# A fused attention and two-layer kernel: attention products three steps later, weight sums in place, output slots and splits at fixed places

## The chip, the cores and the metric

One core of one Trainium2 chip. The metric is the device time of one execution in microseconds (us), the median over the runs. Engines: PE is TensorE's matmul, PEld its weight load, DVE is VectorE, ACT is ScalarE, POOL is GpSimd, SP is SyncE, which issues nearly all DMA transfers here. Each engine works through its own queue in program order.

## What is computed

q, k and v are [8, 8, 576, 64] float32 (drawn as 0.1 times a normal; q and k times about 4.3). Within chunks of 64 rows:

```python
scores = scale * np.matmul(q_c, k_c.transpose(0, 1, 2, 4, 3))
scores = scores - np.max(scores, axis=-1, keepdims=True)
attn = np.exp(scores)
attn = attn / (np.sum(attn, axis=-1, keepdims=True) + 1e-09)
out = np.matmul(attn, v_c)
```

Heads are then laid side by side, which gives x of [4608, 512], and two layers follow, with weights of 512 x 2048 and 2048 x 512 that arrive as float64:

```python
h = x @ w_in                                                # layer one
x = (np.maximum(h, 0.0) + alpha * np.minimum(h, 0.0)) @ w_out
h = x @ w_in2                                               # layer two
out = (h - np.tanh(h)) @ w_out2
```

## The kernel before

**Precision.** Each float32 operand of a large product is split into a high part (a ScalarE copy into float32r, the type that PE takes) and a low part (operand minus high part, on VectorE or GpSimd); a product is hi*hi + lo*hi + hi*lo, three matmuls for one. The float64 weights are turned into float32 by bit operations (`to_f32_a` on ScalarE, L115 and L118; `to_f32_op` on VectorE, L128 to L138).

**Steps (layer one, blocks 0 to 6).** The 4608 tokens form nine blocks of 512. The first seven go through layer one in 112 steps, one for each block and slice of 128 of the 2048 hidden values. A step (`step_one`, L1008 on) holds twelve matmuls `up` (L525) into a PSUM bank `hps` (two exist), the gate (`act_g`: ScalarE L536 and L537, VectorE L538), the split of the last step's gate (L553, L556), and twelve matmuls `down` (L595) for the gate of two steps earlier. Everything else is hung into steps by a table of events: `at(step, fn, ..., place=)`. `fire` runs the places 0 to 4 of a step: 1 and 2 ahead of `up`, 0 between `up` and `down`, 3 after `down`, 4 after the gate. So each engine's queue is written by hand.

**Attention inside the steps.** A tile is 128 tokens with all eight heads. For a tile t with `base[t] = s`: raw q and k come by many small DMAs (`begin_unit`, `some_loads`, L318; for four tiles in the natural layout, L284) and are transposed on VectorE (`att_a`, L363) or, natural ones, on PE; scores at s (`att_s`, L378), maximum, subtraction and exponential at s + 1 (`att_e`), normalization at s + 2 (`att_n`), the transpose of the weights (`att_t`, L428) and their copies into the single buffer `ptb` (`att_d`: four on VectorE, L437, four on ScalarE, L438) at the end of s + 2, and the product with v (`att_v`, L449) at s + 3. One step later the result is copied out as a split operand (`att_x`, L495 and L499) or, for the last two blocks, staged and stored (`att_x_out`, L511). Scores and products share one pair of PSUM banks: the products of one tile stand beside the scores of another (`beside`). The raw buffer is single, and its next loads begin when the last transpose has read it. `base` holds a gap of three steps between most tiles and of four at four places.

**Parked weights.** From step 36 on, in rounds of four steps, seven sums and differences of weight quarters for each pair of hidden slices are formed, split and stored to DRAM (`wu`) for the later cycles, in two halves c = 0 and 1. `park_form` forms layer one's ("u1") from the resident split weights on GpSimd (L215, L221) and layer two's ("u") from a converted raw load; `park_split` splits (L238 on ScalarE, L239 on GpSimd); `park_store` issues two DMAs (L244). Both kinds use the one buffer `mr` of tag "r"; the raw load and the high part take the two buffers of tag "w". In a round the u1 form stands at the end of step 0, its split at the end of step 1, its store in step 2; the u load in step 1, its form at the end of step 2, its split at the end of step 3, its store in step 4. From step 100 on the second layer's `w_out2` slices ("d") follow, six in the steps and ten in the cycles.

**Cycles (`two_blocks`).** The last two blocks of layer one (s = 0) and layer two's blocks in pairs (s = 1 to 4) use seven products for eight: a cycle (s, p) makes p1, p5, p6, p2, p3, p7, p4 (six matmuls each, L1168) for a pair of blocks and a pair of hidden slices. Weights come through a ring of eight buffers (`fetch_up`, L260). VectorE makes the sums H1 = X + p5 and Y = X + p5 in PSUM (`add`, L1175); H1 is the operand of the bank that p3 goes on with. Four gates of a cycle run on ScalarE (`Gate.square`, `second`, `edge`: L568 to L580) and VectorE (`drain`: L573, L574, from PSUM; `close`: L584 to L586, from SBUF). Gated values wait in a list `line` of units, half of them by way of DRAM; `downs(n)` issues n matmuls of the front unit's twelve (L1084). Sizes of these runs are in `gaps`, 24 matmuls a cycle for s = 0 and 48 for s >= 1. A unit's values are split (L553, then L556 on GpSimd) when a unit begins, for the two first of the line, and the third in the middle. When the last unit of a block ends, four banks are copied out (`put_bank`, L620, three buffers of tag "st" in turn) and the next block's first unit begins in the same banks; for s >= 1 that is in the cycles p = 0 and p = 4. `border` hangs the next pair's operands into places of a cycle: loads (`load_y`), differences (`tokens`, L688), split copies (`put`, L676, L678). `small` does the last block at half width. Working buffers of 128 x 512 come from a list of some twenty slots (`take`, first in first out).

## Time and profile before

| what | us |
|---|---|
| runs: median (lowest to highest of 3) | 1808.88 (1802.18 to 1812.13) |
| the profiled execution | 1804.53 |
| its span, first to last instruction | 1802.8 |
| PE / PEld busy | 1656.1 / 1351.9 |
| DVE / ACT / POOL busy | 1302.5 / 994.8 / 469.6 |
| DMA: 276.51 MB moved, mean | 153 GB/s |

The profile is of one execution. Busy time is the union of an engine's instructions. "PEclk" or "clock" is the share of TensorE's full clock (2.4 GHz) that was granted in a stretch; the lower level is 1.2 GHz. A wait is the idle time of an engine before an instruction, put down to what ended it ("<-"). The timeline merges equal instructions in a row (xN). "SPq" are DMA issues on SyncE's queue. A tile's name is that of the program; one name can stand for several buffers.

### The profile page before, as it was taken

The page shows a single profiled execution, that of the slowest core. Times are in us where ns is not written, and L with a number is a line of the kernel's source. Part 1 is how long each engine was busy: PE and PEld are TensorE (multiplying, and loading weights), DVE is VectorE, ACT ScalarE, POOL GpSimd, SP SyncE. Part 2 cuts the span into 40 slices and gives each one's busy share as a digit, 9 for nine tenths or more (in the row PEclk, how much of TensorE's full clock was granted, in tenths as well). Part 3 has the DMA queues.
Part 4 walks back from the last instruction along what each step waited for, and adds up shares of the span by engine and source line. Part 5 has one row for each costly group of instructions (what it writes and reads, how often), then busy time and mean ns, then how long its engine had stood idle before and what let it go on. Part 6 is the DMA issues. An engine that isn't in the chain of part 4 may idle for free.

```text
span 1802.8 us, 26393 instructions
## 1 busy us (share of the span) xinstructions
PE 1656.1 (92%) x9309; PEld 1351.9 (75%) x9309; DVE 1302.5 (72%) x1860; ACT 994.8 (55%) x1785; POOL 469.6 (26%) x406
## 2 busy tenths in 40 slices
...
GB/s 252 184 138 39 97 99 117 128 140 104 136 94 126 128 117 140 154 146 197 230 239 234 292 238 101 185 147 176 111 184 137 176 123 175 136 155 141 224 170 24
DMA packets 345061, 276.51 MB, mean 153 GB/s; under 512 B 180048, under 2 KB 250720, under 8 KB 344928
## 3 DMA queue, kind: packets, MB, share of 16 engines
...
q14 instruction: 59, 0.48, 0.1%
...
## 4 chain that ended last, share of the span: by engine, by line
PE 39%; DVE 12%; DMA 6%; ACT 6%; issue 5%; SPq 3%; POOL 2%; DVEq 0%; ACTq 0%; POOLq 0%
PE y L1084 18%; PE hpb L1168 11%; PE hps L1168 6%; PE y L595 3%; SPq L318 3%; DMA wu<-mr 2%; PE hps L525 2%; DVE arena L585 2%; DVE arena L584 1%; DMA out_dram<-yst 1%; ACT sq L568 1%; DVE arena L573 1%; ACT w L577 1%; DVE th L574 1%; DMA wu<-wu 1%
## 5 line engine op out<-in xcount | busy, mean ns | idle before, releaser
L556 POOL TENSOR_TENSOR glo<-arena,ghi 128x512 fp32r<-128x512 f32 x142 | 206.0, 1455 | 519.0 <-ACT ghi L553 437.2
L525 PE MATMUL hps<-x,w 128*128 128x512 f32 (+1 forms) x1356 | 328.7, 392 | 4.5 <-ACT kt L352 3.8
L1084 PE MATMUL y<-w,ghi 128*128 128x512 f32 x1152 | 301.3, 395 | 10.1 <-ACT yst L620 10.1
L525 PEld LDWEIGHTS hps<-x,w 128*128 128x128 f32 x1356 | 255.8, 190 | 58.8 <-ACT kt L352 4.2
L1168 PE MATMUL hpb<-w,wu 128*128 128x512 f32 (+1 forms) x1200 | 284.4, 380 | 8.5 <-DVE th L574 5.1
L1168 PEld LDWEIGHTS hpb<-w,wu 128*128 128x128 f32 x1200 | 218.5, 190 | 55.5 <-DVE th L574 8.1
L1084 PEld LDWEIGHTS y<-w,ghi 128*128 128x128 f32 x1152 | 217.6, 191 | 56.4 <-ACT yst L620 12.2
L595 PE MATMUL y<-ghi,w 128*128 128x512 f32 x880 | 250.2, 420 | 0.0
L595 PEld LDWEIGHTS y<-ghi,w 128*128 128x128 f32 x880 | 174.5, 203 | 39.0
L1168 PE MATMUL hps<-w,wu 128*128 128x512 f32 (+1 forms) x624 | 143.1, 373 | 25.2 <-DVE hps L1175 24.8
L1084 PE MATMUL y<-w,glo 128*128 128x512 f32 x576 | 163.7, 391 | 0.0
L556 DVE TENSOR_TENSOR glo<-g,ghi 128x512 fp32r<-128x512 f32 x111 | 111.8, 1008 | 68.9 <-ACT ghi L553 68.8
L239 POOL TENSOR_TENSOR mr<-mr,whi 128x896 fp32r<-128x896 f32 (+1 forms) x48 | 93.4, 1946 | 256.1 <-ACT whi L238 247.0
L1168 PEld LDWEIGHTS hps<-w,wu 128*128 128x128 f32 x624 | 109.2, 191 | 52.9 <-DVE hps L1175 33.8
L586 DVE COPY_PREDICATED arena<-ktc,th 128x512 f32<-128x512 uint32 x126 | 132.8, 1054 | 11.4 <-ACT ktc L580 0.6
L538 DVE SCALAR_TENSOR_TENSOR g<-neg,nalpha_sb,g 128x512 f32<-128x512 f32 x112 | 92.5, 826 | 60.2 <-ACT g L537 60.2
L595 PE MATMUL y<-glo,w 128*128 128x512 f32 x440 | 130.2, 400 | 1.0 <-DVE glo L556 1.0
L1084 PEld LDWEIGHTS y<-w,glo 128*128 128x128 f32 x576 | 108.4, 189 | 22.5
L585 DVE SCALAR_TENSOR_TENSOR arena<-sq,arena 128x512 f32<-128x512 f32 x126 | 116.6, 926 | 4.3
L221 POOL TENSOR_TENSOR mr<-mr 128x128 f32<-128x128 f32 x128 | 72.7, 578 | 154.4 <-DVE mr L138 140.0
L536 ACT ACTIVATE neg<-hps 128x512 f32<-128x512 f32 x112 | 65.9, 589 | 75.8 <-PE hps L525 75.1
L577 ACT ACTIVATE w<-sq,bias_sb 128x512 f32<-128x512 f32 x144 | 104.5, 726 | 0.0
...
## 6 DMA issues: line engine op xcount, KB each, us to landing
...
```

Source lines behind the costliest of these rows:

```text
L221: nc.gpsimd.tensor_tensor(out=mr[:, o], in0=mr[:, x], in1=mr[:, y], op=op)
L239: nc.gpsimd.tensor_tensor(out=lo.bitcast(F32R), in0=m, in1=h.bitcast(F32), op=ALU.subtract)
L525: nc.tensor.matmul(out=hp[:, cols], lhsT=w[:, a, m], rhs=x[b][:, kk, cols], start=(kk == 0 and i == 0), stop=(kk == KD - 1 and i == 2),)
L536: nc.scalar.activation(out=neg, in_=hp, func=AF.Relu, scale=-1.0)
L538: nc.vector.scalar_tensor_tensor(out=g, in0=neg, scalar=nalpha_sb[:, f:f + 1], in1=g, op0=ALU.mult, op1=ALU.add)
L556: lo_engine.tensor_tensor(out=lo, in0=g, in1=hi.bitcast(F32), op=ALU.subtract)
L577: nc.scalar.activation(out=self.w, in_=self.sq, func=AF.Square, bias=bias_sb)
L585: nc.vector.scalar_tensor_tensor(out=g, in0=self.sq, scalar=TS[0], in1=g, op0=ALU.add, op1=ALU.mult)
L586: nc.vector.copy_predicated(g, self.mask.bitcast(U32), self.th)
L595: nc.tensor.matmul(out=acc[t], lhsT=lhsT, rhs=rhs, start=(f == ends[0] and i == 0), stop=(f == ends[1] and i == 2))
L1084: nc.tensor.matmul(out=self.acc[t], lhsT=lhsT, rhs=rhs, start=(self.f == self.ends[0] and i == 0), stop=(self.f == self.ends[1] and i == 2),)
L1168: nc.tensor.matmul(out=o, lhsT=w[:, a, c], rhs=x[c][:, b, :h], start=start and i == 0 and c == 0, stop=i == 2 and c == 1, skip_group_check ...
```

## The change

- The products move from s + 3 to s + 6, `att_t` to the beginning and `att_d` to the end of s + 3. `base` becomes an even row of three steps; the transposes of a pair that follows a natural tile begin one step before its scores instead of two.
- u1 sums are formed in a buffer of tag "w". Only four of the seven are formed and split, in place; the three that are plain quarters are stored straight from the resident high and low parts (three more DMAs for each pair, at c = 0). The order of the seven in DRAM differs by layer. A round becomes: load u, form u1 (step 0); split u1, form u (1); split u, and at the end store u1 (2); store u at the end (3).
- "d" slices: the load stands a step ahead of the form; in the cycles the ten are spread evenly, one in 11.5 us of a nominal cycle of 15 us, so that all lie in s = 0.
- Splits of waiting units stand at fixed places of a cycle: up to three after p5, one to three after the square of the last gate; `ready`, `born` and the two clocks go.
- In cycles p = 0 and 4 of s >= 1 the runs of output matmuls become 12 after p5, 12 after p6, 6 after p7, 12 + 6 after p4, from 12, 12 (after p7) and 24.
- The copies of finished banks take a slot instead of a buffer of tag "st".
- Operands of the next pair: most `put` and `tokens` move to the end of a cycle, p5's to after p1.

```diff
-    OPS = {"p1": 0, "p7": 1, "p2": 2, "p4": 3, "p5": 4, "p6": 5, "p3": 6}
+    OPS = (
+        {"p6": 0, "p7": 1, "p3": 2, "p5": 3, "p1": 4, "p2": 5, "p4": 6},
+        {"p1": 0, "p7": 1, "p2": 2, "p4": 3, "p5": 4, "p6": 5, "p3": 6},
+    )
...
-        mr = wide.tile([P, 8, P], F32, tag="r", name="mr", bufs=1)
-        flat = mr.rearrange("p s m -> p (s m)")
         if kind == "u1":
+            mr = wide.tile([P, 8, P], F32, tag="w", name="mw")
...
+            sums = ((3, 1, 3, ALU.add), (1, 0, 1, ALU.subtract), (0, 3, 0, ALU.subtract), (2, 2, 0, ALU.subtract))
         else:
+            mr = wide.tile([P, 8, P], F32, tag="r", name="mr", bufs=1)
+            flat = mr.rearrange("p s m -> p (s m)")
             to_f32_b([to_f32_a(parked[kind, n, c], flat[:, :512], flat.bitcast(I32)[:, 512:])])
-        if kind != "d":
-            for o, x, y, op in ((4, 1, 3, ALU.add), (1, 0, 1, ALU.subtract), (5, 4, 0, ALU.subtract),
-                                (6, 2, 5, ALU.subtract)):
-                nc.gpsimd.tensor_tensor(out=mr[:, o], in0=mr[:, x], in1=mr[:, y], op=op)
+            sums = ((4, 1, 3, ALU.add), (1, 0, 1, ALU.subtract), (5, 4, 0, ALU.subtract), (6, 2, 5, ALU.subtract))
+        for o, x, y, op in sums if kind != "d" else ():
+            nc.gpsimd.tensor_tensor(out=mr[:, o], in0=mr[:, x], in1=mr[:, y], op=op)
...
-        hi = wide.tile([P, 8, P], F32R, tag="w", name="whi")
+        hi = mr.bitcast(F32R) if kind == "u1" else wide.tile([P, 8, P], F32R, tag="w", name="whi")
...
-            m, h, lo = mr[:, 0:7], hi[:, 0:7], mr[:, 0:7]
-            to = [wu[layer, n][:, :, i, c] for i in range(2)]
+            if layer == 0:
+                m, h, lo = mr[:, 0:4], hi[:, 4:8], mr[:, 0:4]
+                to = [wu[0, n][:, 0:4, i, c] for i in range(2)]
+            else:
+                m, h, lo = mr[:, 0:7], hi[:, 0:7], mr[:, 0:7]
+                to = [wu[1, n][:, :, i, c] for i in range(2)]
...
+        if kind == "u1" and c == 0:
+            for o, e, g in ((4, 0, 0), (5, 0, 1), (6, 1, 1)):
+                parked[kind, n, c] += ((
+                    wu[0, n][:, o].rearrange("p u c m -> p u (c m)"),
+                    wsplit[2 * n + e, 0][:, :, g * 256:(g + 1) * 256].bitcast(F32),
+                ),)
...
-            nc.sync.dma_start(out=ring[u % RING].bitcast(F32), in_=wu[layer, n][:, OPS[ORDER[u % 7]]])
+            nc.sync.dma_start(out=ring[u % RING].bitcast(F32), in_=wu[layer, n][:, OPS[layer][ORDER[u % 7]]])
...
-    base.update({
-        12: 28, 13: 31, 14: 35, 15: 38, 29: 41, 30: 44, 16: 47, 17: 50, 18: 53, 19: 56, 31: 59, 20: 63, 21: 66, 22: 69,
-        23: 73, 24: 76, 25: 79, 26: 82, 27: 85, 28: 88, 32: 91, 33: 94, 34: 97, 35: 100,
-    })
+    base.update({t: 28 + 3 * i for i, t in enumerate((
+        12, 13, 14, 15, 29, 30, 16, 17, 18, 19, 31, 20, 21, 22, 23, 24, 25, 26, 27, 28, 32, 33, 34, 35
+    ))})
...
-    free = HF + 3
+    free, apart = HF + 3, 2
...
-            free = base[t]
+            free, apart = base[t], 1
         else:
-            turn = base[t] - (1 if t == 11 else 2)
+            turn, apart = base[t] - (1 if t == 11 else apart), 2
...
-    pv = {t: base[t] + (4 if t < 3 * NPT else 3) for t in order}
+    pv = {t: base[t] + (4 if t < 3 * NPT else 6) for t in order}
...
-            at(s + 2, att_t, t, place=4)
-            at(s + 2, att_d, t, place=4)
+            at(s + 3, att_t, t, first=True)
+            at(s + 3, att_d, t, place=4)
...
-    def park(load, form, kind, n, c):
-        if kind != "u1":
-            at(load, park_load, kind, n, c)
-        at(form, park_form, kind, n, c)
-        at(form + 1, park_split, kind, n, c)
-        at(form + 2, park_store, kind, n, c)
-
     for i in range(KF):
-        step = 2 * KF + 4 + 4 * i
-        park(None, step, "u1", i // 2, i % 2)
-        park(step + 1, step + 2, "u", i // 2, i % 2)
+        n, c, step = i // 2, i % 2, 2 * KF + 4 + 4 * i
+        at(step, park_load, "u", n, c)
+        at(step, park_form, "u1", n, c)
+        at(step + 1, park_split, "u1", n, c)
+        at(step + 1, park_form, "u", n, c)
+        at(step + 2, park_store, "u1", n, c, place=4)
+        at(step + 2, park_split, "u", n, c)
+        at(step + 3, park_store, "u", n, c, place=4)
...
-        park(step, step, "d", f, 0)
+        at(step, park_load, "d", f, 0)
+        at(step + 1, park_form, "d", f, 0, place=2)
+        at(step + 1, park_split, "d", f, 0, place=4)
+        at(step + 2, park_store, "d", f, 0, place=1)
...
+    def split_ahead(n):
+        for u in line[:n]:
+            u.split()
+
...
-                clock[1] += 1
-                for u in line[:2]:
-                    u.split()
+                line[0].split()
...
-            if line[0].at == 4 and len(line) > 2 and line[2].ready():
-                line[2].split()
...
-            return lambda t, a: put_bank(a, ysc[j][t])
+            return lambda t, a: put_away_slot(a, ysc[j][t])
...
-            return lambda t, a: put_bank(a, out[j * NB + t * P:j * NB + (t + 1) * P, :], last=last and t % 2 == 1)
+            return lambda t, a: put_away_slot(a, out[j * NB + t * P:j * NB + (t + 1) * P, :], last and t % 2 == 1)
+
+        def put_away_slot(a, to, last=False):
+            st = take()
+            if last:
+                nc.vector.tensor_copy(st, a)
+            else:
+                nc.scalar.activation(out=st, in_=a, func=AF.Copy)
+            nc.sync.dma_start(out=to, in_=st)
+            slots.append(st)
...
-            line[-1].born -= 1
...
-            on(s, 4, "p7", load_y, m, "b22", "b21")
+            on(s, 5, "start", load_y, m, "b22", "b21")
...
-            on(s, 5, "p7", tokens, m, "b11", "b12", "b11", V)
+            on(s, 5, "end", tokens, m, "b11", "b12", "b11", V)
             on(s, 5, "end", tokens, m, "b12", "b22", "b12", V)
-            on(s, 6, "p7", tokens, m, "e1", "b22", "b11", V)
+            on(s, 6, "end", tokens, m, "e1", "b22", "b11", V)
...
-                (7, "p5", "p5", "b11"), (7, "p6", "p6", "e1"), (7, "p7", "p2", "b21"), (7, "p4", "p3", "b22"),
-                (8, "p1", "p7", "b12"), (8, "p6", "p4", "e2"),
+                (7, "p1", "p5", "b11"), (7, "end", "p6", "e1"), (7, "end", "p2", "b21"), (7, "end", "p3", "b22"),
+                (8, "p1", "p7", "b12"), (8, "p2", "p4", "e2"),
...
+        PLACES = {"start": 0.0, "p1": 1.4, "p5": 2.7, "p6": 4.1, "p2": 5.4, "p3": 6.8, "p7": 8.2, "p4": 12.2, "end": 14.2}
+
+        def when(us, fn, *args):
+            p, us = divmod(us, 15.0)
+            place = max((x for x in PLACES if PLACES[x] <= us), key=PLACES.get)
+            on(int(p) // NPAIR, int(p) % NPAIR, place, fn, *args)
+
+        todo = []
         for i, f in enumerate(range(DP, KF)):
-            s, p = (0, i) if i < 7 else (1, i - 6)
-            on(s, p, "p1", park_load, "d", f, 0)
-            on(s, p, "p7", park_form, "d", f, 0)
-            on(s, p, "end", park_split, "d", f, 0)
-            on(s, p + 1, "start", park_store, "d", f, 0)
-        on(1, 4, "start", parks_done)
+            todo += [(11.5 * i, park_load, f), (11.5 * i + 5.5, park_form, f), (11.5 * i + 8.5, park_split, f),
+                     (11.5 * i + 11.4, park_store, f)]
+        for us, fn, f in sorted(todo, key=lambda x: x[0]):
+            when(us, fn, "d", f, 0)
+        on(1, 0, "start", parks_done)
...
-            clock[0] += 1
-            gaps = (0, 0, 12, 12) if s == 0 else (12, 0, 12, 24) if p % 4 == 0 else (0, 0, 12, 36)
+            turns = s > 0 and p % 4 == 0
+            gaps = (0, 0, 0, 12, 12) if s == 0 else (12, 12, 0, 6, 18) if turns else (0, 0, 0, 12, 36)
...
+            split_ahead(2 if turns or s == 0 else 3)
...
+            downs(gaps[1])
+            if turns:
+                split_ahead(2)
...
-            downs(gaps[1])
+            downs(gaps[2])
...
-            downs(gaps[2])
+            downs(gaps[3])
...
-            downs(min(12, gaps[3]))
+            downs(min(12, gaps[4]))
...
+            if s > 0 or p == NPAIR - 1:
+                split_ahead(1 if s == 0 else 3 if p % 4 == 3 else 2)
...
-            downs(gaps[3] - 12)
+            downs(gaps[4] - 12)
...
-            clock[0] += 1
...
```

Left out are the same moves in the half-width cycles and the removal of `ready`, `born` and the clocks.

## Rows read from the trace of the kernel before

**Rows 1.** The page, part 1: busy us (share of the span) xinstructions

```profile
PE 1656.1 (92%) x9309; PEld 1351.9 (75%) x9309; DVE 1302.5 (72%) x1860; ACT 994.8 (55%) x1785; POOL 469.6 (26%) x406
```

**Rows 2.** PE waits: who, line, on what: us in total, times, longest

```profile
PE sc L449 <- ACT ptb L438: 48.3, 23, 6.2
PE hps L1168 <- DVE hps L1175: 24.8, 16, 2.9
PE xp L449 <- ACT ptb L438: 17.2, 7, 9.5
PE y L1084 <- ACT yst L620: 10.1, 5, 3.6
...
PE sc L378 <- ACT xst L511: 6.8, 1, 6.8
```

**Rows 3.** Windows: us, busy (x) of PE PEld DVE ACT POOL, clock, DMA, GB/s

```profile
236.52:818.60 582.08, 506.28 (x3378) 409.64 (x3376) 368.90 (x572) 263.98 (x489) 178.70 (x197) 0.93 0.48 127
...
950.72:1662.60 711.88, 672.73 (x2882) 544.51 (x2880) 589.59 (x799) 445.40 (x797) 192.61 (x132) 0.99 0.54 170
```

**Rows 4.** Windows: five steps without attention, one with scores and products

```profile
785.94:813.16 27.22, 27.22 (x122) 22.50 (x120) 24.82 (x29) 14.52 (x28) 11.40 (x7) 1.00 0.29 100
341.43:348.19 6.76, 6.76 (x90) 5.45 (x89) 5.23 (x12) 4.39 (x9) 0.90 (x2) 1.00 0.40 72
```

**Rows 5.** Windows: the 17 steps in which PE waits for attention, summed

```profile
sum 223.21, PE 149.63 PEld 116.75 DVE 150.65 ACT 107.36 POOL 73.38; mean PE 8.80 PEld 6.87 DVE 8.86 ACT 6.32 POOL 4.32
```

**Rows 6.** Timeline, step 72: start us, us, engine line op, [idle before <-releaser]

```profile
520.28 0.61 SPq L244 DMA_DIRECT2D wu<-mr  x1
...
526.30 0.66 ACT L115 ACTIVATE mr<-rw 128x512 f32<-128x512 f32 x1 [10.15 <-DMA wu<-mr]
...
534.56 1.70 ACT L438 ACTIVATE ptb<-pt 32x256 f32<-32x256 f32 x4 [5.56 <-DVE pt L428]
...
535.46 0.47 PE L449 MATMUL xp<-ptb,v 64*64 64x64 f32 x2 [9.55 <-ACT ptb L438]
```

**Rows 7.** Windows: a cycle that runs through

```profile
1197.58:1217.98 20.40, 20.40 (x92) 16.90 (x90) 17.35 (x23) 12.50 (x22) 6.28 (x5) 1.00 0.43 129
```

**Rows 8.** Windows: the four cycles p4 of s1 to s4, summed

```profile
sum 98.84, PE 87.77 PEld 70.25 DVE 60.47 ACT 55.64 POOL 21.07; mean PE 21.94 PEld 17.56 DVE 15.12 ACT 13.91 POOL 5.27
```

**Rows 9.** The timeline of cycle s2 p4, at the change of banks

```profile
1237.45 0.60 ACT L620 ACTIVATE yst<-y 128x512 f32<-128x512 f32 x1 [4.63 <-DMA out_dram<-yst]
...
1238.10 1.22 PE L1084 MATMUL y<-w,ghi 128*128 128x512 f32 x2 [2.96 <-ACT yst L620]
```

**Rows 10.** Windows: cycles p5 to p7: two, and the sum of twelve

```profile
1287.29:1313.28 25.99, 22.48 (x92) 17.78 (x90) 23.20 (x33) 16.11 (x29) 6.22 (x4) 0.93 0.40 121
1466.68:1490.02 23.34, 20.85 (x92) 16.63 (x90) 22.12 (x33) 15.96 (x29) 6.36 (x4) 1.00 0.46 136
...
sum 272.35, PE 252.45 PEld 203.80 DVE 245.13 ACT 169.23 POOL 73.00; mean PE 21.04 PEld 16.98 DVE 20.43 ACT 14.10 POOL 6.08
```

**Rows 11.** The timeline of cycle s2 p5, its ends (DVE, POOL, PE)

```profile
1242.97 0.68 DVE L584 SCALAR_TENSOR_TENSOR arena<-w,arena 128x512 f32<-128x512 f32 x1
...
1244.59 1.68 POOL L556 TENSOR_TENSOR glo<-arena,ghi 128x512 fp32r<-128x512 f32 x1 [2.45 <-ACT ghi L553]
...
1245.05 1.76 DVE L584 SCALAR_TENSOR_TENSOR arena<-w,arena 128x512 f32<-128x512 f32 x1
...
1250.23 1.65 PE L1168 MATMUL hps<-w,wu 128*128 128x512 f32 x6 [1.39 <-DVE hps L1175]
...
1263.88 2.99 POOL L556 TENSOR_TENSOR glo<-arena,ghi 128x512 fp32r<-128x512 f32 x2 [3.06 <-ACT ghi L553]
...
1264.32 0.67 DVE L574 TENSOR_TENSOR th<-hpb,th 128x512 f32<-128x512 f32 x1
```

**Rows 12.** Windows: the four cycles p0 of s1 to s4, summed

```profile
sum 90.42, PE 84.95 PEld 68.28 DVE 65.42 ACT 64.10 POOL 23.32; mean PE 21.24 PEld 17.07 DVE 16.35 ACT 16.02 POOL 5.83
```

**Rows 13.** The timeline of cycle s0 p5

```profile
908.30 0.66 ACT L115 ACTIVATE mr<-rw 128x512 f32<-128x512 f32 x1 [3.90 <-issue]
```

15 lines of the change are left out of this document (7 added, 8 removed).

## The prediction, made before the changed kernel ran

> **What bounds the kernel now.** I read the page first: TensorE (PE) is busy for 92% of the span and no other engine for more than 75% [rows 1], so the time is PE's work plus what PE waits for. The waits of PE come next [rows 2]: the largest is the attention product (L449) that waits for ScalarE's copy into `ptb` (L438), 48.3 + 17.2 us in 30 waits; then the third product of a cycle (L1168), 24.8 us for VectorE's sum H1 (L1175), and 10.1 us at a change of output banks for the copy `yst` (L620). Windows by stage tell where they lie [rows 3]. Steps 32 to 111 of layer one (236.52 to 818.60 us) hold 582.08 us with PE idle for 582.08 - 506.28 = 75.8, and a granted clock of 0.93, so a further 0.07 x 582 = 41 us go to running at 1.2 instead of 2.4 GHz: every idle us there costs about 1.5. In cycles s = 1 to 4 (711.88 us) the clock is 0.99, and VectorE is busy for 589.59 us, 83%: the second engine to watch.
>
> **The attention steps.** Five steps without attention take 27.22 us, 5.44 each; a step with the scores of one tile and the products of another takes 6.76, so attention itself costs 1.32 [rows 4]. The 17 steps that wait take 223.21 us [rows 5]; at 6.76 they would take 114.9, so 108.3 us are stall. The timeline of the longest shows its cause [rows 6]: SyncE issues the store of `mr` (a formed sum of layer one) at 520.28, behind a run of raw loads; the converting copy L115 wants the same single buffer of tag "r" and holds ScalarE idle for 10.15 us until that store has landed; VectorE waits behind it; the transpose of the weights, the `ptb` copies (L438, four in 1.70 us) and PE (9.55 us) come last.
>
> The change acts at two places of that chain. The transpose `pt` moves one step and the `ptb` copies to that step's end, and the product moves from three steps after its scores to six. So instead of about half a step there are two steps and more, over 11 us, between the copies and their reader; the longest wait [rows 6] is 9.55. And layer one's sums go from tag "r" to tag "w" and are formed in place, so the conversion no longer wants the buffer whose store has just been issued. What moves along: one VectorE transpose, four copies on VectorE and four on ScalarE, 32 products, one or two loads of `v` on SyncE (they stay three steps ahead of the product), and the copy out with its subtraction or its store, all as many as before; the stores of the sums move on SyncE to the end of a step, behind its loads. The scores now come every three steps throughout, and the last products stay in step 103. All this costs nothing new, since the moved work lands in steps of the same pattern (its period is three steps), under 5.44 us of PE's own work each; were VectorE not done by then, the copies' 1.70 us [rows 6] would be PE's, 23 x 1.70 = 39 us. Three operands of layer one are now stored straight from the resident halves: 24 more issues of some 0.6 us on SyncE [rows 6], 15 us over 350, beside its waits. Still single are `ptb`, `pt` and the pair of score banks: the copies of one tile now follow the products of the one before, which PE issues in the middle of the same step, some 2 us before VectorE gets there.
>
> What is late next: VectorE. Its 368.90 us [rows 3] must fit into the stage without stalls: 80 steps of 5.44, 22 of them with scores and products (+1.32 each), two with products alone and two with natural transposes (about 0.9 each, an estimate from the same 1.32), in all 435.2 + 29.0 + 3.6 = 467.8 us. That is 79% for VectorE, 56% for ScalarE and 38% for GpSimd (178.70, which loses three of seven pieces of every layer one split). It fits, but not everywhere: in the steps after a naturally transposed tile the raw loads of the next pair still have three steps only, and the wait of the scores for `xst` (6.8 us [rows 2]) was not one for `ptb`. GpSimd takes one new wait: its sums now want a "w" buffer whose store was issued a step earlier; its own split and the store behind it on SyncE follow, with a step of slack each. Best case: all 582.1 - 467.8 = 114 us. Worst case that I can price: the waits for `ptb` fall only to a third of 65.5 us, and with the 6.8 us for `xst` 28.6 x 1.5 = 43 us stay, a gain of 71. I take 12 us left (the 6.8 at 1.5, and 2 for the pairs after a natural tile): **-102**, nearer the best end because the new slack exceeds the longest wait on record.
>
> **The cycles.** One that runs through takes 20.40 us [rows 7].
> - p = 4: four take 98.84, 17.2 over [rows 8]. At the change of banks ScalarE idles 4.63 us because the fourth `yst` wants one of three staging buffers whose store must land, and PE waits for it [rows 9]. The change takes the buffer from the list of slots (some twenty, the longest unused first), and three products of hidden values (p2, p3, p7) instead of one (p4) now stand between the last output products of the old block and the first of the new. Bounds: all 17.2, or, should slots run short, nothing. The idle ends with that landing [rows 9], so I take -15.
> - p = 0: 8.8 over [rows 12]; the same change of banks, with a further 12 output products ahead of H1's reader; against it, three operands (six ScalarE copies, six VectorE subtractions) now stand at the end of p = 7. Bounds: +4 (six subtractions of some 0.68 us, as VectorE's ops in [rows 11]) and -8.8; I take -5.
> - p = 5 to 7: twelve take 272.35, 27.5 over [rows 10]. PE waits 1.39 us for H1 [rows 11], since VectorE still closes the last gates. Moving subtractions of tokens from one place to a later one before H1 changes nothing there, as VectorE works through without a pause. What can change is what a split on GpSimd does to it: L584 takes 0.68 us alone and 1.76 where GpSimd's L556 runs [rows 11], while L574, which reads PSUM, takes 0.67 inside such a split. The change puts one split at the end of a cycle, beside ops of that second kind, and up to three after p5, when most closing is done. The cycles p = 7 hold 22 to 23 us of VectorE work [rows 10]; three operands leave them. Bounds: -27 and, if the splits meet the closing, +13 (12 x 1.08, by the same rows). I take -12.
> - s = 1: three conversions of the second layer's weights leave p = 1 to 3 for s = 0. Bounds 0 and -4 (one idle as in [rows 13]); -2.
> - s = 0: a conversion every 11.5 us instead of one a cycle, with its load 5.5 us ahead. Already now ScalarE once idles 3.90 us at such a conversion (L115) [rows 13]; and the last one now stands before H1 in p = 7. Against that, splits come earlier. Bounds: -4 (that idle gone) and +12 (three more like it); I take 0.
> - Half-width cycles and the end: more early splits, no wait removed that I can name: 0.
>
> Sum: -15 - 5 - 12 - 2 = **-34**.
>
> **The sum.** The profiled execution took 1804.53 us (span 1802.8 and 1.7 around it). 1804.53 - 102 - 34 = 1668.5. The median of the runs, 1808.88, stands 4.4 above the profiled one; I forecast 1671 for the median.
>
> **Rivals.**
> *A: the wait moves along.* SyncE's raw loads, the single "r" buffer (now freed by the second layer's own store) and the two "w" buffers keep ScalarE and VectorE behind PE, and PE waits for `glo` or for the bank of hidden products. For it: the chain in rows 6 begins in a queue of loads that is not shortened. Against it: the stores follow their splits a step later, so SyncE stands still less. If half of the 114 us stays, 1804.5 - 57 - 30 + 4 = 1722.
> *B: the cycles give nothing.* The attention gain comes, but slots, splits and conversions only trade places: 1804.5 - 102 + 4 = 1707.
> *C: slower.* Place: after p5, where three copies on ScalarE and three splits on GpSimd come in a row. VectorE's remaining closing ops and token subtractions, which read two SBUF operands, are stretched by 1.76 - 0.68 = 1.08 us for each split [rows 11], 3.2 us in all, and H1 is that late. A wait of 2.49 us with a fallen clock makes a cycle of 25.99, 5.6 over; one without the fall makes 23.34 [rows 10]. With 5.6 in each of 32 cycles: +179 - 102 - 20 = +57, 1866. It decides from 122 / 32 = 3.8 us per cycle on. Against it: the split that now stretches the close at a cycle's end leaves that place.
> The Trainium skill, "SBUF — State Buffer", section "SBUF: two separate sides", says that GpSimd and a VectorE op with two SBUF inputs take one pair of ports in turn, each for its whole instruction. By that rule rival C holds wherever a closing op begins inside a split; the trace agrees on the price, 1.08 us for a split of 1.68, and on L574's freedom from it.
> *D: no change.* VectorE's chain, not PE, sets the pace of the attention steps (368.90 busy of 582.08 and waits in between), and the three steps only lengthen its way: 1809, within 9.
>
> **How the numbers follow.** Forecast 0.62, A 0.18, B 0.12, D 0.03, C 0.05. The forecast's own range is 1640 to 1695 (114 and 50 gained, or 90 and 20); for 8 in 10 the range has to reach A: 1640 to 1724. A measurement of this kernel can tell 0.5% (9 us) from no change. Forecast, A and B are all faster, 0.92; D is the same, 0.03; C slower, 0.05.
>
> **What would show it.** Right: the waits of L449 for `ptb` under 5 us in all, ScalarE's L115 no longer waiting for `wu<-mr`, a clock of 0.99 or more and about 470 to 480 us for steps 32 to 111, no `yst` among PE's waits, cycles p = 4 near 20.5. Wrong: L595 waiting for `glo` or L525 for `neg` in place of L449 (A); H1's waits at L1168 well above 24.8 us (C); L115 waiting for `rw` in s = 0 for more than 10 us, or the stage of steps 32 to 111 above 510 us.

## The result and the profile after

The changed kernel takes **1736.54 us** in the median (1735.33 to 1742.13, 4 runs) beside 1806.88 us for the kernel before on the same chip: a ratio of 0.9616 (95% interval 0.9581 to 0.9651). The forecast was 1671 with a range of 1640 to 1724, so the direction is right and the gain is about half of what was forecast: 70 us of 138. The line numbers of the changed kernel are higher: `up` L539 for L525, `down` L609 for L595, the split L567 and L570 for L553 and L556, products of attention L463 for L449, products of a cycle L1183 for L1168, VectorE's sums L1190 for L1175, `downs` L1091 for L1084.

Page, part 1, of the changed kernel (it answers to [rows 1]); span 1740.4 us:

```profile
PE 1638.2 (94%) x9309; PEld 1339.0 (77%) x9309; DVE 1233.6 (71%) x1860; ACT 994.7 (57%) x1785; POOL 447.5 (26%) x406
```

Windows by stage, of the kernel before (the three stages that rows 3 lack) and of the changed one. In order: steps 0 to 31, steps 32 to 111, s = 0, s = 1 to 4, and the half-width cycles with the end:

```profile
0.00:236.52 236.52, 220.13 (x1782) 181.33 (x1782) 184.59 (x287) 142.76 (x235) 11.18 (x17) 0.97 0.50 137
...
818.60:950.72 132.12, 123.05 (x529) 99.86 (x528) 82.44 (x98) 75.25 (x139) 43.04 (x28) 0.99 0.67 223
...
1662.60:1802.70 140.10, 133.88 (x745) 116.59 (x743) 76.98 (x107) 67.35 (x127) 44.05 (x33) 0.99 0.44 141
```

```profile
0.00:238.31 238.31, 220.66 (x1750) 181.74 (x1750) 183.86 (x286) 142.62 (x234) 6.42 (x11) 0.97 0.49 135
238.31:741.71 503.40, 481.33 (x3409) 389.33 (x3408) 363.34 (x576) 259.59 (x490) 173.31 (x204) 0.98 0.55 147
741.71:898.23 156.52, 130.97 (x530) 104.83 (x529) 78.49 (x108) 79.40 (x146) 43.16 (x30) 0.91 0.65 209
898.23:1585.03 686.80, 665.25 (x2881) 545.05 (x2880) 516.48 (x783) 446.06 (x789) 176.97 (x130) 0.99 0.55 171
1585.03:1740.30 155.27, 139.98 (x745) 118.00 (x743) 91.39 (x111) 67.04 (x127) 47.63 (x33) 0.98 0.40 127
```

Set side by side with [rows 3], this is the whole result:

| stage | before | after | difference | forecast |
|---|---|---|---|---|
| steps 0 to 31 | 236.5 | 238.3 | +1.8 | 0 |
| steps 32 to 111 | 582.1 | 503.4 | -78.7 | -102 |
| s = 0 | 132.1 | 156.5 | +24.4 | 0 |
| s = 1 to 4 | 711.9 | 686.8 | -25.1 | -34 |
| half-width cycles, end | 140.1 | 155.3 | +15.2 | 0 |

Two stages that were costed at nothing became longer by 39.6 us together, and the two that gained gained 32 less than forecast. (Steps 0 to 31 take 235.0 to 238.6 us in the traces of the changed kernel and its edits, which don't differ there, so 1.8 is within their spread.)

The waits of PE in the changed kernel (they answer to [rows 2]):

```profile
PE y L609 <- DVE glo L570: 16.6, 8, 3.1
PE hpb L1183 <- DVE th L588: 15.7, 8, 2.1
PE hps L1183 <- DVE hps L1190: 13.7, 4, 7.3
PE hpb L1183 <- ACT arena L1129: 10.2, 4, 5.0
PE y L1091 <- ACT ghi L567: 9.7, 10, 2.2
```

The largest wait of before, products for `ptb`, is gone from the list. Of the waits for H1 in s = 1 to 4, one of 1.5 us is left of fourteen. These are PE's waits for H1 in that stage, before and after:

```profile
PE hps L1168 <- DVE hps L1175: 20.1, 14, 2.5
```

```profile
PE hps L1183 <- DVE hps L1190: 1.5, 1, 1.5
```

What stands in the list now belongs to four stages: `glo` to the steps, `hps` (12.2 of its 13.7 us) and `arena` to s = 0, `th` to s = 1 to 4, `ghi` to the half-width cycles. Each was followed by experiments.

All kernels that ran, each two to five times beside the kernel before on the same chip, with the stage that each is about (us, from its profiled execution):

| kernel | median | ratio to before (95%) | stage, after | stage, here |
|---|---|---|---|---|
| a_rwfirst | 1718.66 | 0.9504 (0.9477 to 0.9532) | steps 32 to 111: 503.4 | 485.9 |
| a_s0old | 1711.21 | 0.9463 (0.9427 to 0.9499) | s = 0: 156.5 | 129.8 |
| a_s0lead | 1732.01 | 0.9586 (0.9571 to 0.9601) | s = 0 | 149.7 |
| a_s0place | 1730.45 | 0.9564 (0.9544 to 0.9583) | s = 0 | 146.9 |
| a_s0both | 1725.06 | 0.9535 (0.9517 to 0.9553) | s = 0 | 144.3 |
| a_s0lo | 1736.80 | 0.9630 (0.9604 to 0.9656) | s = 0 | 152.9 |
| a_s0lolead | 1722.45 | 0.9543 (0.9523 to 0.9563) | s = 0 | 142.1 |
| a_s0loboth | 1717.27 | 0.9510 (0.9489 to 0.9532) | s = 0 | 133.3 |
| a_smallahead | 1720.67 | 0.9516 (0.9468 to 0.9563) | half-width, end: 155.3 | 137.4 |
| a_oldgaps | 1724.36 | 0.9545 (0.9526 to 0.9564) | s = 1 to 4: 686.8 | 672.5 |
| a_stbank | 1770.32 | 0.9799 (0.9780 to 0.9819) | s = 1 to 4 | 706.5 |
| a_lazy | 1779.78 | 0.9861 (0.9844 to 0.9877) | s = 1 to 4 | 727.6 |
| a_oldborder | 1737.32 | 0.9616 (0.9600 to 0.9632) | s = 1 to 4 | 687.4 |
| b_attn | 1782.73 | 0.9859 (0.9830 to 0.9887) | steps 32 to 111 | 560.6 |
| b_park | 1738.75 | 0.9625 (0.9599 to 0.9650) | steps 32 to 111 | 518.6 |
| a_three | 1673.64 | 0.9270 (0.9253 to 0.9287) | | |
| a_four | 1661.04 | 0.9197 (0.9178 to 0.9217) | | |

Kernels named a_ are edits of the changed kernel, those named b_ edits of the one before. A stage that an edit of the changed kernel does not touch still differs by up to 5 us between the traces: steps 32 to 111 take 500.5 to 504.9 us, s = 0 takes 154.1 to 159.0, s = 1 to 4 take 683.6 to 686.8. Differences of that size in the last column show nothing. The traced execution of the changed kernel, 1742.13 us, is the longest of its four.

### The profile page after: what moved, and what is told of

Its sections match the earlier page's. It is cut to its first block, busy times and chain, and to the rows that moved or that the text cites. A ratio compares the mean times of both kernels' runs of the same rounds, so it can differ in the third digit from the quotient of the medians.

```text
span 1740.4 us, 26381 instructions
## 1 busy us (share of the span) xinstructions
PE 1638.2 (94%) x9309; PEld 1339.0 (77%) x9309; DVE 1233.6 (71%) x1860; ACT 994.7 (57%) x1785; POOL 447.5 (26%) x406
## 4 chain that ended last, share of the span: by engine, by line
PE 59%; DVE 12%; issue 10%; DMA 5%; ACT 5%; SPq 5%; POOL 4%; DVEq 0%; POOLq 0%; ACTq 0%
PE y L1091 19%; PE hpb L1183 13%; PE hps L539 10%; PE y L609 10%; PE hps L1183 5%; DMA rw<-in_moe_w_out_dram 3%; POOL glo L570 2%; SPq L332 2%; DMA wu<-whi 1%; SPq L298 1%; DVE mr L134 1%; DVE arena L587 1%; DVE mr L128 1%; DVE mr L138 1%; DVE glo L570 1%
## 5 line engine op out<-in xcount | busy, mean ns | idle before, releaser
L539 PE MATMUL hps<-x,w 128*128 128x512 f32 (+1 forms) x1356 | 336.0, 398 | 6.2 <-ACT kt L366 5.3
L570 POOL TENSOR_TENSOR glo<-arena,ghi 128x512 fp32r<-128x512 f32 x142 | 197.1, 1402 | 535.9 <-ACT ghi L567 384.7
L1183 PE MATMUL hpb<-w,wu 128*128 128x512 f32 (+1 forms) x1200 | 296.0, 391 | 28.0 <-DVE th L588 11.7
L539 PEld LDWEIGHTS hps<-x,w 128*128 128x128 f32 x1356 | 260.9, 194 | 62.8 <-ACT kt L366 5.8
L1091 PE MATMUL y<-w,ghi 128*128 128x512 f32 x1152 | 298.7, 392 | 9.7 <-ACT ghi L567 9.7
L1183 PEld LDWEIGHTS hpb<-w,wu 128*128 128x128 f32 x1200 | 226.6, 197 | 79.5 <-DVE th L588 14.2
L1091 PEld LDWEIGHTS y<-w,ghi 128*128 128x128 f32 x1152 | 214.9, 189 | 56.3 <-ACT ghi L567 13.5
L609 PE MATMUL y<-ghi,w 128*128 128x512 f32 x880 | 231.4, 395 | 4.2 <-ACT yst L634 3.5
L609 PEld LDWEIGHTS y<-ghi,w 128*128 128x128 f32 x880 | 161.7, 188 | 40.1 <-ACT yst L634 3.9
L1091 PE MATMUL y<-w,glo 128*128 128x512 f32 x576 | 164.7, 392 | 3.4 <-POOL glo L570 3.4
L1183 PE MATMUL hps<-w,wu 128*128 128x512 f32 (+1 forms) x624 | 138.9, 370 | 13.7 <-DVE hps L1190 13.7
L609 PE MATMUL y<-glo,w 128*128 128x512 f32 x440 | 129.7, 399 | 16.6 <-DVE glo L570 16.6
L1183 PEld LDWEIGHTS hps<-w,wu 128*128 128x128 f32 x624 | 111.0, 191 | 35.8 <-DVE hps L1190 15.4
L1091 PEld LDWEIGHTS y<-w,glo 128*128 128x128 f32 x576 | 108.3, 189 | 28.2 <-POOL glo L570 6.0
L567 ACT ACTIVATE ghi<-g 128x512 fp32r<-128x512 f32 x112 | 70.6, 630 | 95.3 <-DVE g L552 95.0
L609 PEld LDWEIGHTS y<-glo,w 128*128 128x128 f32 x440 | 83.0, 190 | 37.3 <-DVE glo L570 20.3
L217 POOL TENSOR_TENSOR mw<-w 128x256 f32<-128x256 f32 x32 | 26.9, 860 | 313.8 <-DMA ysc<-yhalf 235.5
L594 ACT ACTIVATE ktc<-sq,edge_sb 128x512 f32<-128x512 f32 x144 | 103.9, 721 | 0.0
L1193 ACT ACTIVATE hps<-hpb 128x512 f32<-128x512 f32 x40 | 23.3, 582 | 134.4 <-PE hpb L1183 134.4
L599 DVE SCALAR_TENSOR_TENSOR arena<-sq,arena 128x512 f32<-128x512 f32 x116 | 97.0, 836 | 4.0
```

What stands on the lines that cost most here:

```text
L217: nc.gpsimd.tensor_tensor(out=quarters[:, :, e], in0=hi, in1=lo, op=ALU.add)
L539: nc.tensor.matmul(out=hp[:, cols], lhsT=w[:, a, m], rhs=x[b][:, kk, cols], start=(kk == 0 and i == 0), stop=(kk == KD - 1 and i == 2),)
L567: nc.scalar.activation(out=hi, in_=g, func=AF.Copy)
L570: lo_engine.tensor_tensor(out=lo, in0=g, in1=hi.bitcast(F32), op=ALU.subtract)
L594: nc.scalar.activation(out=self.mask, in_=self.sq, func=AF.Relu, bias=edge_sb)
L599: nc.vector.scalar_tensor_tensor(out=g, in0=self.sq, scalar=TS[0], in1=g, op0=ALU.add, op1=ALU.mult)
```

## The experiments

### Which part of the change gave the attention gain

b_attn is the kernel before with the later products alone (new `base`, `pv` and places of `att_t` and `att_d`); b_park is the kernel before with the new handling of parked weights alone (`park_form`, `park_split`, their events, the order in DRAM).

```diff
+    pv = {t: base[t] + (4 if t < 3 * NPT else 6) for t in order}      # b_attn
...
+            at(s + 3, att_t, t, first=True)
+            at(s + 3, att_d, t, place=4)
...
+            mr = wide.tile([P, 8, P], F32, tag="w", name="mw")        # b_park, for "u1"
```

> The kernel before with the attention moves alone: products six steps after the scores, transpose and copies of the weights a step later, scores every three steps. Theory 4: the slack alone takes away the waits for ptb, but the conversions still wait for the store of the sums (the single buffer of tag r), so a part comes back as waits for glo. Then steps 32 to 111, 582.1 us before and 503.4 in the changed kernel, come to 515 to 545 and L115 still waits for wu<-mr by 30 us or more. Rival a: the buffer is the whole cause; then 560 or more. Rival b: the slack is the whole cause; then 500 to 508, as in the changed kernel.

> The kernel before with the new parking of the sums alone (layer one's in a buffer of tag w and in place, four of seven; rounds of load and form, split and form, split and store, store); attention, conversions of w_out2, splits and slots as before. The run with the attention moves alone left steps 32 to 111 at 560.6 us (582.1 before, 503.4 in the changed kernel). Theory 5: the two parts are not additive, each hides the other's gain; the parking takes the conversion's wait for the store away, but the product still stands half a step behind its copies, so 530 to 560 us. Rival a: the parking alone is the cause; then 500 to 512. Rival b: it gives nothing alone; then 572 or more.

PE's waits in steps 32 to 111, of b_attn and then of b_park:

```profile
PE y L595 <- ACT ghi L553: 33.4, 14, 8.7
PE y L595 <- DVE glo L556: 18.0, 14, 3.1
```

```profile
PE sc L463 <- ACT ptb L452: 17.8, 19, 5.2
PE xp L463 <- ACT ptb L452: 8.4, 5, 4.6
```

In b_attn the waits for `ptb` are gone and PE waits for the split of the gate instead; the stage falls by only 21.5, to 560.6, where the theory wanted 545 at most; that is the number of rival a, the buffer. The cause upstream is untouched, as ScalarE's waits of the same stretch show:

```profile
ACT mr L115 <- DMA wu<-mr: 61.1, 12, 8.2
```

In b_park that row does not exist. A part of the waits for `ptb` stays (26.2 of 65.5), and the stage falls by 63.5, to 518.6: less than the 530 to 560 of the theory, not as low as the rival's 512. So most of the gain comes from the new handling of parked weights. That the single "r" buffer is what counts in it is borne out by the row that went; the rest of b_park (four sums for seven, another order within a round, stores at the end of a step) was not tried by itself. The two parts add up roughly: 21.5 + 63.5 = 85.0 against 78.7 together.

### What is left in the attention steps

a_rwfirst issues layer two's raw load ahead of its step's attention loads instead of behind them.

```diff
-        at(step, park_load, "u", n, c)
+        at(step, park_load, "u", n, c, place=1)
```

> The changed kernel with the raw load of a layer two slice moved ahead of the raw attention loads of the same step on SyncE's queue (place 1 instead of 2), nothing else. Theory 2: what is left of the stall in steps 32 to 111 (503.4 us against 468 without) comes from that load being issued behind up to 16 raw loads; the conversion L115 waits for it (26.7 us in 6 waits, up to 6.9) and PE for glo behind it. Then L115's waits for rw fall under 8 us, PE's for glo from 16.6 to under 6, and the stage to 475 to 488 us. Rival: VectorE is simply too full there, or the load's own 5.3 us to landing is the limit; then the stage changes by less than 5 us.

The timeline of the changed kernel shows the wait (SP's, ACT's and PE's rows):

```profile
496.22 9.26 SPq L332 DMA_DIRECT2D raw<-in_k_dram  x16
505.53 0.45 SPq L201 DMA_DIRECT2D rw<-in_moe_w_in_dram  x1
...
510.59 0.66 ACT L115 ACTIVATE mr<-rw 128x512 f32<-128x512 f32 x1 [6.87 <-DMA rw<-in_moe_w_in_dram]
...
517.64 1.19 PE L609 MATMUL y<-glo,w 128*128 128x512 f32 x4 [3.13 <-DVE glo L570]
```

Sixteen issues of raw `k` keep SyncE for 9.26 us; the load behind them reaches its reader 5.06 us after its issue, ScalarE has idled for 6.87, and VectorE's low part and PE follow. Over the stage ScalarE waits so six times, 26.7 us, each time for a load issued behind 10 or more raw loads. With the load first the stage's row is

```profile
235.11:721.02 485.91, 475.04 (x3409) 386.61 (x3408) 368.50 (x576) 260.98 (x490) 172.86 (x204) 0.99 0.57 152
```

17.5 us less, at a clock of 0.99, and within 5.8 of the forecast's 582.1 - 102 = 480.1. PE's waits for `glo` in the stage fall from 16.6 to 9.5 us, where under 6 was expected; the stage hits its range. This load is most of what the forecast lacked here. It binds only with both parts in place: in b_park ScalarE waits for it once, 1.9 us.

### Why s = 0 became 24 us longer

First the old spread: one conversion of `w_out2` a cycle, seven in s = 0 and three in s = 1.

```diff
+            s, p = (0, i) if i < 7 else (1, i - 6)
+            on(s, p, "p1", park_load, "d", f, 0)
+            on(s, p, "p7", park_form, "d", f, 0)
+            on(s, p, "end", park_split, "d", f, 0)
+            on(s, p + 1, "start", park_store, "d", f, 0)
```

> The changed kernel with the ten conversions of w_out2 in the cycles back at their old places (one a cycle, load after p1, form after p7; seven in s = 0, three in s = 1). Theory 1: the even spread of 11.5 us made s = 0 slower, because a load that lies only 5.5 us ahead holds ScalarE and the form then stands before a sum in PSUM. Then s = 0, which went from 132.1 to 156.5 us, comes back to 130 to 136, s = 1 loses up to 3 us, and the whole falls by 18 to 24 us, to about 1716. Rival: the earlier splits or the slots slow s = 0; then it stays at 150 or more and the time at 1733 to 1742.

s = 0 falls to 129.8, a little more than was expected, while s = 1 stays (169.7 for 170.8): the spread is the cause. What of it costs the time? Timeline of the changed kernel, cycle s0 p4 (SP, ACT, DVE, PE):

```profile
809.27 0.38 SPq L258 DMA_DIRECT2D wd<-mr  x1
809.74 0.46 SPq L106 DMA_DIRECT2D rw<-in_moe_w_out_dram  x1
...
815.46 0.67 ACT L115 ACTIVATE mr<-rw 128x512 f32<-128x512 f32 x1 [1.04 <-DMA rw<-in_moe_w_out_dram]
...
816.16 0.43 DVE L128 TENSOR_SCALAR mr<-mr 128x512 f32<-128x512 f32 x1 [5.85 <-ACT mr L115]
...
819.37 0.69 DVE L1190 TENSOR_TENSOR hps<-hpb,ptb 128x512 f32<-128x512 f32 x1
820.11 0.79 PE L1183 MATMUL hps<-w,wu 128*128 128x512 f32 x1 [3.60 <-DVE hps L1190]
```

Three things come together. The load of this conversion was issued 5.7 us before it is used. The store that reads the single "r" buffer (`mr`), which the conversion writes, was issued 0.47 us before that. And the conversion stands ahead of H1 (L1190) in VectorE's queue, so H1 and PE wait behind it. In this cycle the load came last: it landed at 815.36, the store at 814.29, so an earlier load alone could have gained little more than 1 us here. Five edits, alone and together, take the three away: the load 4 us of nominal time earlier; the four conversions at p1, p5 and p3 moved behind H1 or Y; the low part written into the unused half of the high part's buffer, so that the store no longer reads `mr`.

```diff
-            todo += [(11.5 * i, park_load, f), ...
+            todo += [(max(0, 11.5 * i - 4), park_load, f), ...                       # lead
...
+            t = {1: 20.5, 5: 65.5, 8: 98.2, 9: 110.5}.get(i, 11.5 * i + 5.5)         # place
...
-            m, h, lo = mr[:, 0:4], hi[:, 0:4], mr[:, 4:8]
+            m, h, lo = mr[:, 0:4], hi[:, 0:4], hi.bitcast(F32)[:, 4:8]               # buffer
```

> The changed kernel with one edit: in s = 0 each of the ten w_out2 loads is issued 4 us of nominal time earlier, 9.5 instead of 5.5 ahead of its conversion; forms and splits stay where they are. Theory (the stage s = 0 is 24 us longer than before because a conversion waits some 7 us for a load issued too shortly ahead of it, and VectorE and PE wait behind ScalarE): the waits of L115 for rw fall from 20.8 us to under 6, s = 0 takes 136 to 146 us instead of 156.5, the median is 1717 to 1728. Rival (it is the even spread itself: ten forms in s = 0 instead of seven, some of them ahead of H1 on VectorE): s = 0 stays at 150 or more although the waits for rw go, the median is 1731 or more.

Half a hit for either side: ScalarE's waits for `rw` go (20.8 to 1.1 us), but others of 8.6 us come in their place (the row names `wu<-wu`), the stage falls only to 149.7, and the median, 1732.01, lies in the rival's range.

> The changed kernel with one edit in s = 0: the four conversions of w_out2 that stand at p1, p5 or p3 (the second, sixth, ninth and tenth), ahead of VectorE's sum H1 or Y, are formed at p2 or p7, behind it; all ten stay in s = 0 and the loads stay where they are. Theory (place: the forms ahead of the sums make PE wait): PE's waits for H1 and Y at L1183 fall under 8 us in s = 0, the stage takes 132 to 142 us instead of 156.5, the median is 1713 to 1724. Rival (number: ten forms for seven are too much for VectorE in a stage of 130 us): 147 or more, wherever they stand.

> The same with the loads 4 us of nominal time earlier as well. Theory (place first, then the load): the stage takes 130 to 138 us, about that of one conversion a cycle (129.8), the median is 1711 to 1720. Rival (number): 145 or more. If only the load mattered once the places are right, this run is over 5 us below the one with the places alone.

Both miss the theory's ranges and stop just short of the rival's: 146.9 and 144.3. In a_s0place PE's waits for the two sums fall to 6.9 us, as expected, without the stage following. The cycle p4 is repaired (21.77 us to 14.96 and 15.11), p5 to p7 are not (65.55 us to 63.95 and 65.23). The timeline of a_s0both showed why (SP and ACT):

```profile
827.89 0.32 SPq L258 DMA_DIRECT2D wd<-mr  x1
...
833.76 0.66 ACT L115 ACTIVATE mr<-rw 128x512 f32<-128x512 f32 x1 [7.35 <-DMA wu<-wu]
```

The load had been issued at 822.21, 11.5 us earlier; the last thing that the conversion wanted was the store of the previous one, issued 5.87 us before it (the trace has the store's landing at 833.69, 0.07 us ahead of the conversion; the load had landed at 829.10; the row names a load of the ring, which the conversion does not read). That is the mechanism of [rows 6], in another stage. Hence the third edit:

> The changed kernel with one edit: the low part of a w_out2 slice is written into the unused half of its high part's buffer instead of back into mr, so the store no longer reads the single r buffer and the next conversion need not wait for it to land; number, places and loads stay. Theory (a conversion wants mr about 6 us after the store that reads it was issued; load and store come within half a us of each other, so that a trace names only the later): alone it gives 2 to 8 us, since the load is as late: s = 0 at 149 to 154 us, the median 1729 to 1735. Rival (the store of mr does not bind): 155 or more, 1735 or more.

> The same, with the loads 4 us earlier as well: both that a conversion waits for are now out of the way, only the places ahead of the sums stay. Theory: s = 0 at 138 to 145 us, under the run with the loads alone (149.7) by 5 or more; the median 1718 to 1727. Rival: 148 or more.

> The same with the four conversions behind the sums too: all three suspected causes gone, still ten conversions in s = 0. Theory (the single buffer, the late load and the places make up the 24 us, the number nothing): s = 0 at 130 to 136 us, against 129.8 with seven conversions and 144.3 with the loads and places alone; p5 to p7 of it under 56; the median 1710 to 1718. Rival (number): 141 or more.

All three stages fall within the theory's ranges: 152.9, 142.1 and 133.3 (p5 to p7 of the last take 56.55, just over the 56 expected). The median of a_s0lo, 1736.80, does not: it is no better than the changed kernel's, and lies in the rival's range. From the changed kernel on: the load -6.8 (156.5 to 149.7), the buffer a further -7.6 (to 142.1), the places a further -8.8 (to 133.3). The order matters, since one cause hides another: the places alone gave 9.6, and the buffer alone 3.6, which is within this stage's spread. The 3.5 us that remain against the old spread are open; they may be the three conversions more, which was not tried by itself.

### Why the half-width cycles became longer

Before, a unit's splits ran for the first two of the line whenever a unit began; the change splits only the front unit there, and has three fixed places besides. a_smallahead splits two again, in the half-width cycles alone, and takes out the three fixed places there.

```diff
-                line[0].split()
+                split_ahead(look[0])
...
+            look[0] = 2
...
-            split_ahead(2)
...
```

> The changed kernel with the half-width cycles back to splitting the first two units of the line whenever a unit begins, instead of at three fixed places and otherwise only at a unit's own beginning. Theory 3: the third unit of a cycle meets no fixed place, so PE waits 0.8 us for its high part in nearly every cycle (L1091 for ghi 9.7 us, for glo 3.4 in all). Then the last stretch (p = 0 of the half-width cycles to the end) goes from 155.4 to 140 to 143 us and those waits nearly vanish. Rival: the slots for the last output copies or the new stores cost the time; then it stays above 150.

Timeline row of PE in the changed kernel, which comes in most of these cycles, and the stage's row in a_smallahead:

```profile
1615.21 1.19 PE L1091 MATMUL y<-w,ghi 128*128 128x512 f32 x4 [0.81 <-ACT ghi L567]
```

```profile
1584.97:1722.35 137.38, 133.60 (x745) 116.62 (x743) 79.15 (x111) 67.11 (x127) 46.33 (x33) 0.99 0.45 144
```

137.4 us, 17.9 less, 2.7 under the kernel before and below the 140 to 143 expected; PE has no wait left in the stretch. The rule of splits is the whole cause, and the slots for the last output copies, which a_smallahead keeps, are not. The edit brings the second unit back and drops the fixed places at once, so the two were not told apart.

### What gave and took in s = 1 to 4

Windows of the changed kernel, cycles p0, p4, and p5 to p7, summed over s = 1 to 4 (they answer to [rows 12], [rows 8] and [rows 10]):

```profile
sum 96.46, PE 83.97 PEld 66.36 DVE 67.82 ACT 66.21 POOL 28.96; mean PE 20.99 PEld 16.59 DVE 16.96 ACT 16.55 POOL 7.24
```

```profile
sum 89.80, PE 82.24 PEld 66.82 DVE 48.53 ACT 59.70 POOL 20.10; mean PE 20.56 PEld 16.71 DVE 12.13 ACT 14.93 POOL 5.02
```

```profile
sum 251.96, PE 250.46 PEld 206.47 DVE 213.08 ACT 168.91 POOL 64.60; mean PE 62.62 PEld 51.62 DVE 53.27 ACT 42.23 POOL 16.15
```

p5 to p7 gain 20.4 and now take 251.96, 7 over twelve cycles of 20.40 (all 7 in the four cycles p5; p6 and p7 take 20.40 each); p4 gains 9.0; p0 loses 6.0; p1 to p3 gain 1.7. Four edits take the parts back one at a time.

```diff
-            gaps = ... (12, 12, 0, 6, 18) if turns else ...      # a_oldgaps
+            gaps = ... (12, 0, 0, 12, 24) if turns else ...
...
-            st = take()                                          # a_stbank
+            st = stage.tile([P, 512], F32, tag="st", name="yst")
...
-            split_ahead(2 if turns or s == 0 else 3)             # a_lazy: for s >= 1 the old
...
-                line[0].split()                                  #   rule in downs
+                split_ahead(2 if lazy[0] else 1)
...
-            on(s, 5, "end", tokens, m, "b11", "b12", "b11", V)   # a_oldborder, and so on
+            on(s, 5, "p7", tokens, m, "b11", "b12", "b11", V)
```

> The changed kernel with the runs of output matmuls in the cycles p = 0 and 4 of s >= 1 as before: 12 after p5, 12 after p7, 12 and 12 after p4 (the change: 12, 12 after p6, 6 after p7, 12 and 6). In the changed kernel p = 0 takes 2.1 to 4.3 us more than 20.40, p = 4 2.05, and p1 and p5 wait 1.9 to 2.1 us at their first product for the last gate. Theory 6: the short run of 6 at the end causes the wait of p1 and p5; with 12 there it goes (7 waits, about 14 us with the clock), while p = 0 and 4 may take a wait at p3; s1 to s4 together 674 to 682 instead of 686.8. Rival: the new runs are the better ones; s1 to s4 go to 690 or more.

> The changed kernel with the copies of finished banks back in the three buffers of tag st. Theory 7: the fourth copy waits again for a landing store; PE waits for yst 2.5 to 3.6 us in the cycles with p = 4 and one p = 0, and s1 to s4 grow by 10 to 18 us from 686.8. Rival: with three products between the blocks the store has landed in time anyway; then the change is under 4 us and the slots were worth nothing.

> The changed kernel, but in cycles s >= 1 the units are split as before: the first two of the line whenever an output product begins a unit or goes on, the third in a unit's middle when it is ready; s = 0 and the half-width cycles as changed. Theory (the splits at fixed places, up to three after p5 and the rest after the last gate's square, brought the gain in p5 to p7, by taking a split out of the closing of the gates): s = 1 to 4 take 700 to 715 us instead of 686.8, and PE's waits for H1 (hps before L1183) come back by 10 us or more; the median is 1750 to 1765. Rival (the gain there came from moving the next pair's operands): s = 1 to 4 change by less than 6 us, the median is 1731 to 1743.

> The changed kernel, but the next pair's operands for s >= 1 stand at the places of before (p1, p5, p6, p7 and p4 instead of mostly the cycle's end). Theory (fixed splits brought the gain, the borders little): s = 1 to 4 take 688 to 698 us, the median is 1737 to 1748. Rival (the borders brought it): 703 or more, the median 1752 or more. If moving them cost time, 683 or less.

The rows of the four for s = 1 to 4, in this order:

```profile
893.37:1565.84 672.47, 658.10 (x2882) 540.79 (x2881) 526.38 (x782) 440.77 (x789) 180.33 (x129) 1.00 0.56 175
```

```profile
904.36:1610.84 706.48, 670.98 (x2881) 544.56 (x2880) 516.98 (x782) 446.16 (x789) 177.34 (x129) 0.99 0.53 167
```

```profile
895.80:1623.40 727.60, 677.98 (x2882) 552.17 (x2880) 598.42 (x781) 442.72 (x789) 191.57 (x128) 0.97 0.51 162
```

```profile
895.91:1583.32 687.41, 666.91 (x2882) 544.61 (x2880) 520.38 (x786) 445.86 (x789) 173.01 (x130) 0.99 0.54 171
```

a_lazy lies beyond the upper end of its range (700 to 715), a_oldborder is 0.6 under its own and a_oldgaps 1.5 under; a_stbank pays more than was expected, and its list of PE's waits names `th`, not `yst`, in this stage. The new run sizes cost 14.3 us: with the old ones the stage is the shortest of these. The reason stands in the changed kernel's timeline, at the first product after a turn of banks, and in the window of the cycle that begins there:

```profile
1177.49 2.60 PE L1183 MATMUL hpb<-xo,wu 128*128 128x512 f32 x6 [1.89 <-DVE th L588]
```

```profile
1177.49:1199.62 22.13, 22.13 (x91) 18.15 (x91) 18.91 (x29) 13.08 (x23) 3.94 (x4) 0.92 0.36 108
```

Only six output matmuls are left behind the last gate of such a cycle where twelve were; six of the 90 in a cycle of 20.40 [rows 7] are about 1.4 us, and the next cycle's first product waits for VectorE to drain that gate from the bank. Behind such a wait the cycle can run slower with PE busy throughout: this one takes 22.13 us at a granted clock of 0.92, 1.7 more than 20.40, so a wait of 1.9 cost 3.6. That is so in five of the eight cycles behind a turn. With the old sizes PE has no wait for `th` in this stage; it waits 11.1 us for `ghi` instead, in eight waits.

The slots for finished banks are worth 19.7 us here (706.5 without them). That edit reaches s = 0 too, whose banks go the same way: the stage takes 162.5 us there, 6.0 more, and 3.5 more than in any kernel that doesn't touch it. The borders come to 0.6 in all, but two effects cancel in it: with the old places p0 takes 90.5 us instead of 96.5, as before the change, and p5 to p7 take 258.5 instead of 252.0. So moving the operands cost p0 6.0 and gave p5 to p7 6.5, all of it in p7.

The splits at fixed places are worth 40.8, more than the whole gain of the stage, and 28.8 of it lies in p5 to p7 (280.8 with the old rule). The waits for H1 come back with it:

```profile
PE hps L1193 <- DVE hps L1200: 22.7, 14, 3.4
```

With the old rule the stage takes 727.6, longer than before the change. The new run sizes, which stay, may account for p0 (102.2 us for 90.4), but not for p5 to p7, which they leave alone and which take 8.5 more than before; that is open. The four don't add up to the net 25.1 (40.8 + 19.7 + 0.6 - 14.3 = 46.8). A late split and a late bank may stop PE in the same cycles; no run took two of these parts away at once.

How a split place acts is seen in VectorE's groups for s = 1 to 4 (line, shapes, count | busy us, mean ns | idle): before, after and a_lazy.

```profile
L586 DVE COPY_PREDICATED arena<-ktc,th 128x512 f32<-128x512 uint32 x111 | 120.5, 1085 | 9.6
...
L574 DVE TENSOR_TENSOR th<-hpb,th 128x512 f32<-128x512 f32 x64 | 43.6, 682 | 0.0
```

```profile
L600 DVE COPY_PREDICATED arena<-ktc,th 128x512 f32<-128x512 uint32 x103 | 78.1, 758 | 8.7
...
L588 DVE TENSOR_TENSOR th<-hpb,th 128x512 f32<-128x512 f32 x64 | 44.0, 687 | 0.0
```

```profile
L600 DVE COPY_PREDICATED arena<-ktc,th 128x512 f32<-128x512 uint32 x101 | 127.7, 1265 | 8.4
...
L588 DVE TENSOR_TENSOR th<-hpb,th 128x512 f32<-128x512 f32 x64 | 43.5, 680 | 0.0
```

The same closing copy takes 1085, 758 and 1265 ns on average; the drain of a gate from PSUM keeps its 680 to 687 in all three. VectorE's busy time in this stage falls from 589.59 to 516.48 us with the change and is 598.42 with the old rule. The Trainium skill, "SBUF — State Buffer", section "SBUF: two separate sides", says that GpSimd and a VectorE operation with two SBUF inputs lock each other out of shared ports. These rows agree with it: the copy, with its inputs in SBUF, is stretched by up to 507 ns on average, the drain from PSUM is not.

### The repairs together

a_three is the changed kernel with the old spread in s = 0, the load first, and two units of look-ahead in the half-width cycles; a_four has the old run sizes as well.

> The changed kernel with the three edits together: conversions of w_out2 at their old places, the raw load first on SyncE's queue, splits two units ahead in the half-width cycles. Each alone took 26.7, 17.5 and 17.9 us from its own stage. They lie in different stages, so theory: they add up, s = 0 at 128 to 132, steps 32 to 111 at 484 to 490, the last stretch at 136 to 140, the time 1670 to 1682. Rival: an earlier end of one stage upsets the next; then 1690 or more.

> Four repairs of the changed kernel together: w_out2 conversions in s = 0 as before, layer two's raw load ahead of the attention loads, two splits of look-ahead in the half-width cycles, and the old sizes of the output runs in cycles p = 0 and 4. Theory (the four act in different stages and add up): 1673.6 - 14 = 1655 to 1664, with s = 1 to 4 at 664 to 674. Rival (the old sizes only paid where something else was late): 1669 or more.

Both fall into the ranges: 1673.64 and 1661.04 us. Alone they took 26.7 (s = 0), 17.5, 17.9 and 14.3 us from their own stages, 76.4 in all; together 75.5. They add up, as they lie in different stages. Windows of a_four for steps 32 to 111, s = 0, s = 1 to 4 and the end:

```profile
236.58:720.98 484.40, 473.14 (x3410) 385.51 (x3408) 367.12 (x576) 260.92 (x490) 174.06 (x204) 0.99 0.57 153
720.98:850.72 129.74, 122.65 (x529) 100.36 (x528) 67.20 (x96) 74.06 (x137) 36.94 (x28) 0.97 0.67 227
850.72:1522.28 671.56, 658.39 (x2882) 540.59 (x2881) 533.48 (x795) 445.09 (x798) 184.72 (x132) 1.00 0.56 180
1522.28:1660.00 137.72, 133.60 (x745) 116.60 (x743) 79.18 (x111) 67.10 (x127) 46.34 (x33) 0.99 0.44 144
```

PE is busy for 97% of a_four's span, and its median is below the changed kernel's by 1736.54 - 1661.04 = 75.5 us.

## Why the prediction was right and wrong

**What bounds the kernel** was read rightly: nearly all of the gain is PE's idle time of [rows 2] and the clock that it cost. In steps 32 to 111 PE's idle time falls from 75.8 to 22.1 us, and its busy time, at a clock of 0.98 for 0.93, by 25.0.

**The attention steps**, -102 forecast, -78.7 measured, within the bounds of 71 to 114. The chain of [rows 6] was right: L115 no longer waits for `wu<-mr`, no product waits for `ptb`. Wrong is the reason for taking a value near the best end, "because the new slack exceeds the longest wait on record": b_attn, which has that slack, gains 21.5, and b_park, without it, 63.5. The slack moves the stop from `ptb` to the gate's split; the new handling of parked weights takes most of it away. The step that failed is "All this costs nothing new": it followed the stores through SyncE's queue, but not layer two's raw load, which is issued behind ten raw loads or more wherever it is waited for. Its price, 17.5 us, is most of the gap of 23.3. Rival A named this form (a wait for `glo` in place of `ptb`, SyncE's loads as the cause) and overrated it: it left 57 of 114 us standing, where 503.4 - 467.8 = 35.6 stood and the load made half of that. That the measured 1736.5 lies nearer A's 1722 than the forecast's 1671 is chance: more than half of the gap arose in s = 0 and the half-width cycles, of which A says nothing.

**s = 0**, 0 forecast (-4 to +12), +24.4 measured. The step that failed is the term for a conversion every 11.5 us, whose bounds were taken from the idle of [rows 13]. That idle was taken as the price of one late load. But in the new spread the load and the store of the single "r" buffer are issued within half a microsecond of each other, some 6 us ahead of the conversion, and several conversions, not only the last one, stand ahead of VectorE's sums. The text had the second half ("the last one now stands before H1 in p = 7") and left it out of the bounds. The row of [rows 6] had already shown the price of the first: a store of `mr` just issued holds L115 until it lands. Taken away one after the other, load, store and places gave back 23.2 of the 24.4.

**Half-width cycles**, 0 forecast, +15.2 measured. The step that failed is "more early splits, no wait removed that I can name": in these cycles the change removes the second unit from the look-ahead and adds places elsewhere. The diff says so; it was not followed into this stage.

**s = 1 to 4**, -34 forecast, -25.1 measured. p5 to p7: -12 forecast, -20.4 measured; the mechanism was right, but it was priced by one closing line (L584, 1.08 us, twelve times), while over the stage the two behind it were stretched more: the means fall from 761 to 711 ns for L584, from 883 to 749 for L585 and from 1085 to 758 for L586. That moving subtractions of tokens changes nothing in these cycles was wrong too: a_oldborder puts that at 6.5 us, in p7. p4: -15 forecast, -9.0 measured; the wait for `yst` is gone, but one for `th`, 1.9 us, stands there in each. p0: -5 forecast (bounds -8.8 and +4), +6.0 measured. The step that failed in both is the shift of output matmuls, counted only for what it does ahead of H1 and at the change of banks; nothing was charged for the shorter run behind the last gate, which costs 14.3 over the stage (3.8 of it in p4, 4.1 in p0). In p0 the operands that moved cost a further 6.0, more than the +4 they were given. s = 1: -2 forecast; p1 to p3 of all four gained 1.7.

**Signs.** Of those named as right, L449 and L115 came as said and `yst` left the cycles; the clock (0.98), the stage (503.4) and p4 (22.45) missed. Of those named as wrong, two showed: L609 waiting for `glo`, and L115 waiting for `rw` in s = 0 for 20.8 us. Rival C did not occur: there is one H1 wait in s = 1 to 4, of 1.5 us. Rivals B and D fall with the two gains.

**The sum.** The sum of the prediction gives 1668.5 + 4.4 = 1672.9 for the median; the 1671 that it states is 1.9 lower, and in the changed kernel the median stands 5.6 below the profiled execution, not 4.4 above. With the terms as measured the forecast of the profiled execution would have been 1668.5 + 23.3 + 24.4 + 15.2 + 8.9 + 1.8 = 1742.1, which is what it took; this only shows that no stage was left out. The range missed since the two stages costed at 0 had bounds of -4 to +12, and none.
